# A fused two-layer kernel: the order of its instructions now comes from a list scheduler

## The chip, the cores and the metric

The kernel runs on one NeuronCore of a Trainium2 chip. The metric is the time of one execution on the device in microseconds (us); less is better. TensorE (PE) does the matrix products into PSUM banks, VectorE (DVE), ScalarE (ACT) and GpSimd (POOL) do elementwise work, and SyncE (SP) issues the DMA transfers. Each engine works through its own instructions in a fixed order; semaphores tie the engines together.

## The reference

Three steps on 16384 tokens (4 x 4096) of width 192:

```python
out = np.einsum('hk,bskhg->bshg', softmax(weight), x_unf)  # causal window of 7 taps, 8 heads of 24
h = x @ w_in                 # layer 1: 192 -> 2048
x = (h * np.cos(h)) @ w_out  # back to 192
h = np.maximum(x @ w_in2, 0) # layer 2, the same sizes
y = (h * h) @ w_out2
```

`x` is float32, the four weight matrices are float64.

## The kernel before, in words

Tokens are handled in `NB` = 32 blocks of `T` = 512 columns, the hidden width in `NC` = 16 chunks of 128. Every operand of a product is split into a high and a low part of the type float32r, and each product is done as high x high + high x low + low x high. The width 192 is cut into 128 + 64 rows (`P`, `R`).

One item is one chunk of one block in one layer. Its first products (IN) fill a PSUM bank `h`. In layer 1 ACT rounds it (`kf1`), DVE subtracts (`f1`), ACT takes the sine (`sin1`), DVE multiplies by `h` (`g1`), ACT casts the high part (`hi1`), and DVE or POOL subtracts the low part (`lo1`). In layer 2 ACT does relu, square and the cast (`relu2`, `sq2`, `hi2`) and DVE the low part (`lo2`). The second products (OUT) add the item into two banks `o`, which `evac` scales, splits and passes on (layer 1) or sends out (layer 2) once the block's 16 chunks are in.

The seven taps of a block (`conv_ops`) run on DVE; for block 0 they are shared with ACT and POOL. A chunk's weights are loaded and split in seven steps, `prep_m` to `prep_l`: bit masks and arithmetic on DVE (lines 181 to 183 and 194), the exponent on ACT, the product on POOL (200), the cast on ACT or DVE (206, 208, 209), the subtractions on POOL or DVE (219, 220, 226, 227).

Two kinds of TensorE instruction matter. An unpaired product (`mm_in`, `mm_out`, lines 293 to 303) uses all 128 rows of the array; an item costs 5 + 5 of them. A paired one (`MIX`, line 349) uses 64 rows, and two of them, for the lower and the upper half, run side by side; two items, one of each layer, cost 9 + 10 such pairs. The semaphore `turns` keeps the halves of one bank in order.

The order is written by hand: the string `START` up to the first product, then the lists of `PHASES`, one pass per step `s`. Steps 0 to 15 take block 0 through layer 1; from step 26 (`DEL`) layer 2 follows; from step 42 on `MIX` pairs one item of each layer, and after step 511 layer 2 goes on alone, unpaired, for its last 26 chunks. All weights are split before step 42.

Of the kernel before, what the change touches and what calls it, by code (L numbers as in the profile page):

```python
# [22 lines left out]
P = 128  # L23
# [4 lines left out]
DEL = 26  # L28
CUT = (320, 224)
SPLIT = ("A", "G")  # L30
BUFS = {"raw": 3, "s": 3, "m": 4, "k": 2, "g": 3, "r": 3, "g1": 3, "g2": 3, "o": 4, "h": 4}

START = (
    "X m@V:0 X Y X Y p:0 S X S Y s@V:0 S X Y S X S Y X w@V:0 m@V:1 Y S h@V:0 Y p:1 s@V:1 X S S Y "
    "d@V:0 l@V:0 m@V:2 S p:2 s:2 w@G:1 m@V:3 h:1 p:3 S S S d:1 l:1 w:2"
)

PHASES = (
    (
        0,  # L40
        "IN1:0 k1:0 s@V:-3 w@G:-3 f1:0 OUT1:2 h@A:-2 m:-4 hi1:1 F sin1:0 d:-2 p:-4 lo1@G:1 "
        "l:-2 g1:0",
    ),
    (
        16,
        "p:5 IN1:-2 s:-2 k1:-1 F d@G:-2 f1:-1 sin1:0 hi1:1 lo1@G:1 w@G:-1 OUT1:2 F l@G:-3 "
        "h@V:0 g1:0 m:3",
    ),
    (
        22,  # L50
        "w@G:-2 IN1:-1 k1:-1 f1:-1 F IN2:0 p:-3 relu2:0 hi1:1 h@V:-2 sq2:0 d@G:-2 sin1:-1 OUT1:2 m:-4 "
        "l@G:-2 s@V:-3 hi2:0 lo2@V:0 g1:0 lo1@G:1 OUT2:1",
    ),
    (
        42,
        "MIX k1:0 hi1:1 F Ea f1:0 relu2:-1 sin1:0 sq2:-1 hi2:0 lo2:0 lo1:1 hi2:-1 g1:0 F Es",
    ),
)


def f32(t):
    return t.bitcast(F32)


@with_exitstack
def tile_kernel(
# [22 lines left out]
    g_p = ctx.enter_context(tc.tile_pool(name="g", bufs=BUFS["g"]))
    r_p = ctx.enter_context(tc.tile_pool(name="r", bufs=BUFS["r"]))  # L90
    g1_p = ctx.enter_context(tc.tile_pool(name="g1", bufs=BUFS["g1"]))
    g2_p = ctx.enter_context(tc.tile_pool(name="g2", bufs=BUFS["g2"]))
    ps_h = ctx.enter_context(tc.tile_pool(name="ps_h", bufs=BUFS["h"], space=PSUM))
    ps_o = ctx.enter_context(tc.tile_pool(name="ps_o", bufs=BUFS["o"], space=PSUM))
# [60 lines left out]
    IH, OA, OX, IL, OL, IX = 0, P, 2 * P, 3 * P, 4 * P, 5 * P  # L155
    WC = 6 * P
    wts = [const.tile([P, NC, WC], F32R, name=f"wt{l}") for l in (1, 2)]
    srcs = (w1, w2)
    HALF = -1
    FULL = ((IH, "xh"), (IH, "xl"), (IL, "xh"), (IX, "yh"))  # L160
    U = 2 * D
    lower, upper = slice(0, R), slice(R, P)
    prep = {}

    def prep_load(u):

        l, c = divmod(u, NC)
        raw = raw_p.tile([P, U, 2], I32, tag="raw", name="raw")
        nc.sync.dma_start(raw[:, : P + D], srcs[l][c * P : (c + 1) * P, : P + D])
        for half, d in ((lower, c & ~1), (upper, c | 1)):  # L170
            row = d * P + c % 2 * R
            nc.sync.dma_start(raw[half, P + D :], srcs[l][row : row + R, P + D :])
        prep[u] = raw

    def prep_m(u, E=V):

        raw = prep[u]
        hi, lo = raw[:, :, 1], raw[:, :, 0]
# [12 lines left out]

    def prep_s(u, E=V):
        raw, s, m = prep[u]
        E.scalar_tensor_tensor(  # L194
            out=s, in0=raw[:, :, 1], scalar=-(2**31), in1=s, op0=ALU.bitwise_and, op1=ALU.bitwise_or
        )

    def prep_w(u, E=G):
        raw, s, m = prep[u]
        E.tensor_tensor(out=f32(m), in0=f32(m), in1=f32(s), op=ALU.mult)  # L200

    def prep_h(u, E=A):
        l, c = divmod(u, NC)
        w = f32(prep[u][2])
        t = wts[l][:, c, :]
        (E.copy if E is A else E.tensor_copy)(t[:, 0 : P + D], w[:, 0 : P + D])
        even, odd, x = rest(l, c)
        A.copy(even[lower, x], w[lower, P + D :])
        A.copy(odd[upper, x], w[upper, P + D :])

    def rest(l, c):
        x = IX + c % 2 * R
        return wts[l][:, c & ~1, :], wts[l][:, c | 1, :], slice(x, x + R)

    def prep_d(u, E=V):
        l, c = divmod(u, NC)
        w = f32(prep[u][2])
        even, odd, x = rest(l, c)
        E.tensor_tensor(out=even[upper, x], in0=w[lower, P + D :], in1=f32(even[lower, x]), op=ALU.subtract)
        E.tensor_tensor(out=odd[lower, x], in0=w[upper, P + D :], in1=f32(odd[upper, x]), op=ALU.subtract)  # L220

    def prep_l(u, E=G):
        l, c = divmod(u, NC)
        w = f32(prep.pop(u)[2])
        t = wts[l][:, c, :]
        E.tensor_tensor(out=t[:, IL:IX], in0=w[:, 0 : 2 * P], in1=f32(t[:, 0 : 2 * P]), op=ALU.subtract)
        E.tensor_tensor(
            out=t[:, OX + R : IL], in0=w[:, 2 * P : P + D], in1=f32(t[:, OX : OX + R]), op=ALU.subtract
        )


    xin = {}
    x1 = {}
    x2 = {}
    ready = [0, 0]

    def is_ready(l):
        ready[l] += 1

    def load_x(n):  # L240
        x = xin_p.tile([P, 2, T + PAD], F32, name="x")
        nc.sync.dma_start(x, xp[:, n])
        xin[n] = x[:, 0], x[:, 1]

    def conv_ops(n):

        src = xin.pop(n)
        parts = []
        ops = []
        for j in range(2):  # L250
            y = y_p.tile([P, T], F32, tag=f"y{j}", name=f"y{j}")
            h = x1_p.tile([P, T], F32R, tag=f"xh{j}", name=f"xh{j}")
            lo = x1_p.tile([P, T], F32R, tag=f"xl{j}", name=f"xl{j}")
            parts.append((h, lo))

            def tap(k, E=V, c=slice(0, T), y=y, j=j):
                xk = src[j][:, k + c.start : k + c.stop]
                wk = wtap[:, j, k : k + 1]
                if k == 0:
                    E.tensor_scalar(y[:, c], xk, wk, None, op0=ALU.mult)  # L260
                else:
                    E.scalar_tensor_tensor(out=y[:, c], in0=xk, scalar=wk, in1=y[:, c], op0=ALU.mult, op1=ALU.add)  # L262

            def both(k, tap=tap, cut=CUT[j], y=y, j=j):
                if cut < T:
                    xk = src[j][:, k + cut : k + T]
                    z = y[:, cut:] if k == 0 else r_p.tile([P, T], F32, tag="r", name="z")[:, cut:]
                    A.activation(z, xk, AF.Copy, scale=wtap[:, j, k : k + 1])
                    if k > 0:
                        G.tensor_tensor(out=y[:, cut:], in0=y[:, cut:], in1=z, op=ALU.add)  # L270
                if cut > 0:
                    tap(k, V, slice(0, cut))

            def last(y=y, h=h, lo=lo, c=SPLIT[0] if n == 0 else "V", d=SPLIT[1] if n == 0 else "V"):
                (A.copy if c == "A" else V.tensor_copy)(h, y)  # L275
                engines[d].tensor_tensor(out=lo, in0=y, in1=f32(h), op=ALU.subtract)  # L276

            f = both if n == 0 else tap
            ops += [lambda k=k, f=f: f(k) for k in range(K)] + [last]
        x1[n] = parts  # L280
        ops[-1] = lambda f=ops[-1]: (f(), is_ready(0))
        return ops


    def mm_in(h, l, c, parts, todo):
        w = wts[l][:, c, :]
        (xh, xl), (yh, yl) = parts
        for o, x, st, sp in todo:
            x = {"xh": xh, "xl": xl, "yh": yh, "yl": yl}[x]
            k = slice(0, P)  # L290
            if o == HALF:
# [381 lines left out]
```

## Time and profile before

| what | value |
|---|---|
| time, median of 3 runs | 2418.58 us (2416.64 to 2419.15) |
| the profiled execution: its time, its span | 2418.69 us, 2416.9 us |
| PE busy | 2318.7 us, 96% of the span |
| DVE busy, ACT busy, POOL busy | 1871.2, 1910.1, 158.3 us |
| chain that ended last | PE 90%, DVE 6%, ACT 2% of the span |

The span runs from the first instruction to the last. A share over the whole span mixes stages with different limits, so the rows below are read by stage: the opening up to about 261 us, the paired stretch, and the unpaired end from 2346 us.

### The profile page before, as it was taken

To read this page: it belongs to the slowest core of one execution; us is meant where nothing else is said; L and a number is where in the kernel's file an instruction comes from. 1 tells how busy PE (TensorE), PEld (TensorE's weight loads), DVE (VectorE), ACT (ScalarE), POOL (GpSimd) and SP (SyncE) were. 2 spreads that over 40 slices of the span, in tenths; PEclk is the share of its full clock that TensorE was granted. 3 is DMA by queue.
4 is the path that set the end of the run, shared out by engine and by line. 5 is a ranking of instruction groups with operands and counts; after the bars stand their busy time and mean duration, and the time that the engine had idled before them with its cause. 6 is when DMAs were issued, how large, how long until landed. Compare 5 with 4: busy or idle time off the path is not lost.

```text
span 2416.9 us, 45917 instructions
## 1 busy us (share of the span) xinstructions
PE 2318.7 (96%) x18682; PEld 1999.2 (83%) x18682; DVE 1871.2 (77%) x3036; ACT 1910.1 (79%) x3361; POOL 158.3 (7%) x186
## 2 busy tenths in 40 slices
PE   3578999999999999999999999999999999999999
PEld 2456788888888888888888888888888888888887
DVE  8988778777777887777888777788777778777653
ACT  4556788888888888888888888888888788888877
POOL 5557100000000000000000000000000000000000
PEclk8889999999999999999999999999999999999999
DMA  2211000000000000000000000000000000000000
GB/s 90 62 40 55 16 17 17 1 17 17 17 17 17 12 6 17 17 17 17 17 6 13 16 17 17 17 17 6 12 17 17 17 17 17 1 17 17 8 8 14
DMA packets 21859, 45.10 MB, mean 19 GB/s; under 512 B 3216, under 2 KB 7312, under 8 KB 21648
## 3 DMA queue, kind: packets, MB, share of 16 engines
q1 hardware_dynamic: 21648, 42.16, 5.7%
q8 instruction: 148, 2.42, 0.4%
q14 instruction: 63, 0.52, 0.1%
HBM read 29.56 MB, written 12.58 MB: 17 GB/s over the span
## 4 chain that ended last, share of the span: by engine, by line
PE 90%; DVE 6%; ACT 2%; issue 1%; POOL 0%; DMA 0%; ACTq 0%; DVEq 0%
PE o L349 45%; PE h L349 41%; PE h L293 2%; DVE y L262 1%; DVE g L466 1%; ACT k L452 1%; DVE raw_m L182 1%; DVE raw_s L194 1%; DVE gl L498 1%; DVE raw_s L181 1%; DVE k L458 0%; PE o L300 0%; PE o L302 0%; PE o L303 0%; PE o L301 0%
## 5 line engine op out<-in xcount | busy, mean ns | idle before, releaser
L349 PE MATMUL o<-gh,wt 64*128 64x512 f32 x5628 | 1008.7, 392 | 0.0
L349 PE MATMUL h<-xh,wt 64*128 64x512 f32 x2814 | 954.1, 392 | 3.0 <-DVE xh L275 1.8
L349 PE MATMUL h<-x2h,wt 64*128 64x512 f32 x1876 | 736.6, 393 | 0.7 <-ACT r L484 0.7
L349 PE MATMUL o<-gl,wt 64*128 64x512 f32 (+1 forms) x3752 | 700.9, 392 | 0.0
L452 ACT ACTIVATE k<-h,quarter 128x512 int32<-128x512 f32 x512 | 352.6, 689 | 427.4 <-PE h L349 342.3
L349 PEld LDWEIGHTS o<-gh,wt 64*128 64x128 f32 x5628 | 592.6, 184 | 94.4 <-issue 5.5
L458 DVE TENSOR_TENSOR k<-h,k 128x512 f32<-128x512 f32 x512 | 353.1, 690 | 352.7 <-ACT k L452 346.6
L349 PE MATMUL h<-xl,wt 64*128 64x512 f32 x1407 | 551.4, 392 | 0.2 <-DVE xl L276 0.2
L349 PEld LDWEIGHTS h<-xh,wt 64*128 64x128 f32 x2814 | 517.4, 184 | 36.9 <-DVE xh L275 2.2
L462 ACT ACTIVATE k<-k,right 128x512 f32<-128x512 f32 x512 | 369.2, 721 | 21.4 <-DVE k L458 21.3
L498 DVE TENSOR_TENSOR gl<-r,gh 128x512 fp32r<-128x512 f32 x512 | 353.3, 690 | 41.1 <-ACT gh L492 39.9
L349 PEld LDWEIGHTS h<-x2h,wt 64*128 64x128 f32 x1876 | 345.8, 184 | 45.9 <-ACT r L484 1.0
L349 PEld LDWEIGHTS o<-gl,wt 64*128 64x128 f32 (+1 forms) x3752 | 347.5, 158 | 42.8
L349 PE MATMUL h<-y2h,wt 64*128 64x512 f32 x938 | 368.5, 393 | 0.0
L349 PE MATMUL h<-x2l,wt 64*128 64x512 f32 x938 | 368.4, 393 | 0.0
L466 DVE TENSOR_TENSOR g<-k,h 128x512 f32<-128x512 f32 x512 | 348.7, 681 | 0.4
L492 ACT CAST gh<-r 128x512 fp32r<-128x512 f32 x512 | 317.8, 621 | 15.7
L477 DVE TENSOR_TENSOR gl<-g,gh 128x512 fp32r<-128x512 f32 x471 | 322.6, 685 | 0.0
L488 ACT ACTIVATE r<-r 128x512 f32<-128x512 f32 x512 | 320.4, 626 | 1.1
L471 ACT CAST gh<-g 128x512 fp32r<-128x512 f32 x512 | 312.7, 611 | 5.8 <-DVE g L466 5.6
L484 ACT ACTIVATE r<-h 128x512 f32<-128x512 f32 x512 | 308.0, 602 | 4.7 <-PE h L293 4.6
L262 DVE SCALAR_TENSOR_TENSOR y<-x,wtap,y 128x512 f32<-128x512 f32 (+1 forms) x384 | 295.1, 770 | 5.1
(90 smaller groups left out, 2100.4 us busy)
## 6 DMA issues: line engine op xcount, KB each, us to landing
x<-in_xp_dram SPq DMA_DIRECT2D x32, 518.0 KB, 3.7
raw<-in_w_dram SPq DMA_DIRECT2D x32, 320.0 KB, 2.9
out_dram<-ac SPq DMA_DIRECT2D x32, 256.0 KB, 2.0
out_dram<-bc SPq DMA_DIRECT2D x32, 128.0 KB, 2.3
raw<-in_w_dram SPq DMA_DIRECT2D x64, 32.0 KB, 2.6
w_sm<-in_wrep_dram SPq DMA_DIRECT2D x1, 7.0 KB, 1.7
```

Source lines behind the costliest of these rows:

```text
L262: E.scalar_tensor_tensor(out=y[:, c], in0=xk, scalar=wk, in1=y[:, c], op0=ALU.mult, op1=ALU.add)
L349: return nc.tensor.matmul(bank[0:m], w[k, o : o + m], x[k], start=st, stop=sp)
L452: A.activation(k, h_t[0, i], AF.Identity, bias=quarter)
L458: V.tensor_tensor(out=f, in0=h_t[0, i], in1=k, op=ALU.subtract)
L462: A.activation(tmp[i], tmp[i], AF.Sin, scale=2.0 * math.pi, bias=right)
L466: V.tensor_tensor(out=g, in0=tmp.pop(i), in1=h_t.pop((0, i)), op=ALU.mult)
L471: A.copy(h, tmp[i])
L477: E.tensor_tensor(out=lo, in0=tmp.pop(i), in1=f32(h), op=ALU.subtract)
L484: A.activation(r, h_t.pop((1, i)), AF.Relu)
L488: A.activation(tmp2[i], tmp2[i], AF.Square)
L492: A.copy(h, tmp2[i])
L498: E.tensor_tensor(out=lo, in0=tmp2.pop(i), in1=f32(h), op=ALU.subtract)
```

## The change: two blocks side by side, weights two chunks at a time, one scheduler

All work is now described as steps (`Step`) with a cost on each engine that may do it, the steps they follow, the buffers they take and free, and a due time. `Order.run` takes, over and over, the step that can start first on its engine by these costs, the earlier due one at a tie, and emits it. The costs are numbers in the code; the chip then works through what was emitted.

```diff
-DEL = 26
-CUT = (320, 224)
-START = (
...
-PHASES = (
...
+LEAD = 4
+EARLY = 3
+LAGS = (3, 2)
+BUFS = {"raw": 2, "s": 2, "m": 2, "x": 3, "t": 12, "g": 11, "h": 4, "o": 4, "xs": 4}
+PAIR, DRAIN, WAY = 233, 170, 90
...
+    def run(self):
...
+                    at = max(now, s.ready)
+                    for kind, n in s.takes:
...
+                        key = (at, s.due, s.seq)
+                        if pick is None or key < pick[0]:
+                            pick = key, s
```

A step of the weights now handles two chunks, 768 columns instead of 384, and all of its arithmetic is on DVE and ACT. A pair comes in by seven DMAs.

```diff
-    U = 2 * D
+    U = 2 * (P + D) + P
...
+        b = order.add(
+            "s" + name,
+            {"V": one(U)},
...
+            "p" + name,
+            {"A": act(U)},
...
+            "m" + name,
+            {"V": one(U)},
...
+            "f" + name,
+            {"V": two(U)},
...
+            "n" + name,
+            {"V": two(U)},
...
+            "w" + name,
+            {"V": two(U)},
...
+            "h" + name, {"A": act(U)}, lambda s, e: A.copy(w[:, HI : HI + U], f32(m())), (g2,), due=due - 2500
...
+        return order.add("l" + name, {"V": two(U) + 300}, low, (h,), frees=((d, "m"),), due=due - 1500)
```

The functions behind these names are those of before on wider tiles, and `low` makes three subtractions, of 640, 64 and 64 columns (lines 337, 340 and 341). Blocks 0 and 1 go through layer 1 together. A slot takes one item of the list `first` and one of `other`, pairs their first products (6 + 3 pairs) and the second products of two earlier items (5 + 5 pairs). Two items of one layer can now be a pair, since a pair needs an even and an odd chunk only.

```diff
+    first = [(0, 0)] + [(0, n) for n in range(2, NB)] + [(1, NB - 1)]
+    other = [(0, 1)] + [(1, n) for n in range(NB - 1)]
+    xs = [Item(l, n, c, i * NC + c) for i, (l, n) in enumerate(first) for c in range(NC)]
+    ys = [Item(l, n, c ^ 1, i * NC + c) for i, (l, n) in enumerate(other) for c in range(NC)]
...
+        if x < LEAD:
+            ins = (0, xs[x]), (0, xs[x + 1])
+            x += 2
+        elif x == late and y < late + LEAD:
+            ins = (1, ys[y]), (1, ys[y + 1])
+            y += 2
+        elif x == late and pend[0]:
+            pass
+        elif x < len(xs) and y < len(ys):
+            ins = (0, xs[x]), (1, ys[y])
+            x, y = x + 1, y + 1
...
+            {"V": 685, "G": pool(T)} if it.slot < 18 and it.n == 1 else {"V": 685},
...
+        p = product(f"IN{turn}", 6 if turn == 0 else 3, write, after, (("h", 2),) if turn == 0 else (), done)
...
+        p = product(f"OUT{turn}", 3 if x is y else 5, write, after, (("o", 2 * len(new)),) if new else (), frees)
```

On DVE, before, in the opening, one chunk's weights (`raw_s`, `raw_m`, `wt`) stand between the steps of one item at a time (`k` and `g`, with a tap `y`):

```order
L181 TENSOR_SCALAR raw_s<-raw 128x384
L182 TENSOR_SCALAR raw_m<-raw 128x384
L183 SCALAR_TENSOR_TENSOR raw_m<-raw,raw_m 128x384
L262 SCALAR_TENSOR_TENSOR y_266<-x,wtap,y_266 128x512
L219 TENSOR_TENSOR wt_108<-raw_m,wt_108 64x64
L220 TENSOR_TENSOR wt_108<-raw_m,wt_108 64x64
L466 TENSOR_TENSOR g<-k,h_473 128x512
L194 SCALAR_TENSOR_TENSOR raw_s<-raw,raw_s 128x384
L458 TENSOR_TENSOR k<-h_514,k 128x512
```

On DVE, now, at the fifth of the sixteen pairs of chunks (line 603 is the old `f1`, 617 the old `g1`, 648 the old `lo1` and `lo2`; `t` and `g` are shared buffers):

```order
L302 SCALAR_TENSOR_TENSOR m_72<-raw_68,m_72 128x768
L648 TENSOR_TENSOR g_90<-t_88,g_93 128x512
L311 SCALAR_TENSOR_TENSOR s_70<-raw_68,s_70 128x768
L603 TENSOR_TENSOR t_85<-h_100,t_85 128x512
L326 TENSOR_TENSOR m_72<-m_72,s_70 128x768
L603 TENSOR_TENSOR t_77<-h_101,t_77 128x512
L617 TENSOR_TENSOR t_86<-t_85,h_100 128x512
L648 TENSOR_TENSOR g_95<-t_81,g_94 128x512
L337 TENSOR_TENSOR wt_66<-m_72,wt_66 128x640
L340 TENSOR_TENSOR wt_66<-m_72,wt_66 128x64
L341 TENSOR_TENSOR wt_66<-m_72,wt_66 128x64
```

The product (326) and the large subtraction (337), which POOL did, now stand on DVE, twice as wide, and the steps of two items come between them.

On PE, before, in the opening, the second products of one chunk of block 0 follow the first products of another (`h`, `o` banks, `xh` and `xl` the parts of the block):

```order
L293 MATMUL h_555<-xh_140,wt_108 128x512
L293 MATMUL h_555<-xl_141,wt_108 128x512
L293 MATMUL h_555<-xh_140,wt_108 128x512
L293 MATMUL h_555<-xh_143,wt_108 128x512
L293 MATMUL h_555<-xl_144,wt_108 128x512
L299 MATMUL o_360<-gh_542,wt_108 128x512
L300 MATMUL o_360<-gl_549,wt_108 128x512
```

On PE, now, in an early slot, the halves of two items alternate, here in the second turn of the first products and the start of the second products (`xs` 108 to 111 are the parts of block 0, 112 to 115 those of block 1):

```order
L411 MATMUL h_101<-xs_112,wt_66 128x512
L411 MATMUL h_100<-xs_108,wt_66 128x512
L411 MATMUL h_101<-xs_113,wt_66 128x512
L411 MATMUL h_100<-xs_109,wt_66 128x512
L411 MATMUL h_101<-xs_112,wt_66 128x512
L411 MATMUL h_100<-xs_108,wt_66 128x512
L411 MATMUL o_106<-g_96,wt_66 128x512
L411 MATMUL o_104<-g_90,wt_66 128x512
```

Each product of before is now half of a pair with a product of another block, on the same pair of weight chunks.

## Rows read from the trace of the kernel before

**Rows 1.** Busy time by stage: stretch, its length, each engine, PEclk, DMA.

```profile
0.00:30.00 30.00, 2.83 (x4) 1.34 (x5) 26.65 (x59) 11.78 (x26) 16.32 (x24) 1.00 0.36 115
30.00:140.00 110.00, 70.41 (x224) 49.94 (x224) 100.75 (x155) 63.17 (x128) 61.24 (x63) 0.84 0.17 52
140.00:261.00 121.00, 97.15 (x355) 71.04 (x353) 94.56 (x158) 76.40 (x159) 80.74 (x100) 0.92 0.16 47
261.00:294.00 33.00, 30.62 (x245) 25.76 (x247) 25.33 (x42) 24.28 (x43) 0.00 (x0) 0.95 0.10 29
294.00:2346.00 2052.00, 2052.00 (x17580) 1798.52 (x17576) 1597.14 (x2585) 1682.14 (x2920) 0.00 (x0) 1.00 0.05 14
2346.00:2417.00 71.00, 65.69 (x282) 52.56 (x280) 26.77 (x41) 52.35 (x88) 0.00 (x0) 1.00 0.04 12
```

**Rows 2.** The chain that ended last: start, length, engine, tile, line, count.

```profile
2344.99 1.17 PE o L349 x10
...
2411.45 0.25 PE o L303
...
2412.99 0.68 DVE bc L426
```

**Rows 3.** Groups of instructions, mostly of the weights: count, busy, mean ns, idle.

```profile
L200 POOL TENSOR_TENSOR raw_m<-raw_m,raw_s 128x384 f32<-128x384 f32 x31 | 32.3, 1043 | 28.8 <-DVE raw_s L194 28.8
...
L226 POOL TENSOR_TENSOR wt<-raw_m,wt 128x256 fp32r<-128x256 f32 x31 | 27.3, 882 | 3.1 <-ACT wt L206 1.8
L194 DVE SCALAR_TENSOR_TENSOR raw_s<-raw,raw_s 128x384 int32<-128x384 int32 x32 | 24.7, 771 | 0.0
L183 DVE SCALAR_TENSOR_TENSOR raw_m<-raw,raw_m 128x384 f32<-128x384 uint32 x32 | 22.3, 696 | 1.1
...
L182 DVE TENSOR_SCALAR raw_m<-raw 128x384 int32<-128x384 int32 x32 | 20.4, 639 | 0.0
L419 ACT COPY sw<-bc 64x512 f32<-64x512 f32 x32 | 19.8, 620 | 0.4
...
L181 DVE TENSOR_SCALAR raw_s<-raw 128x384 int32<-128x384 int32 x32 | 16.4, 513 | 0.0
```

**Rows 4.** DVE in order of time in the opening: start, length, instruction.

```profile
86.86 1.42 DVE L182 TENSOR_SCALAR raw_m<-raw 128x384 int32<-128x384 int32 x1
...
92.96 0.35 DVE L181 TENSOR_SCALAR raw_s<-raw 128x384 int32<-128x384 int32 x1
93.23 0.36 DVE L182 TENSOR_SCALAR raw_m<-raw 128x384 int32<-128x384 int32 x1
93.62 0.56 DVE L183 SCALAR_TENSOR_TENSOR raw_m<-raw,raw_m 128x384 f32<-128x384 uint32 x1
94.09 1.77 DVE L262 SCALAR_TENSOR_TENSOR y<-x,wtap,y 128x512 f32<-128x512 f32 x1
```

**Rows 5.** POOL in order of time, the same stretch.

```profile
86.68 1.38 POOL L477 TENSOR_TENSOR gl<-g,gh 128x512 fp32r<-128x512 f32 x1
```

**Rows 6.** DVE in order of time in the paired stretch.

```profile
1002.24 0.68 DVE L498 TENSOR_TENSOR gl<-r,gh 128x512 fp32r<-128x512 f32 x1
...
1003.44 0.68 DVE L466 TENSOR_TENSOR g<-k,h 128x512 f32<-128x512 f32 x1
1004.04 1.53 DVE L262 SCALAR_TENSOR_TENSOR y<-x,wtap,y 128x512 f32<-128x512 f32 x2
```

**Rows 7.** PE alone in short stretches: length, busy (count), PEclk, DMA.

```profile
78.00:82.00 4.00, 3.82 (x9) 0.50 0.31 88
285.00:287.00 2.00, 0.50 (x2) 0.95 0.00 0
287.00:289.00 2.00, 1.88 (x10) 0.50 0.00 0
289.00:291.00 2.00, 2.00 (x16) 0.70 0.00 0
```

**Rows 8.** DMA issues on the page: KB each, us to landing.

```profile
x<-in_xp_dram SPq DMA_DIRECT2D x32, 518.0 KB, 3.7
```

More of the change, by code (lines that the diff above doesn't have):

```diff
@@ L1 @@
+import heapq
 import math
-from collections import deque
 from contextlib import ExitStack
@@ new lines, with __init__, add, open @@
+class Order:
+    def __init__(self):
+        self.steps = []
+        self.free = {}
+        self.hold = {}
+    def add(self, *a, **k):
+        s = Step(*a, **k)
+        s.seq = len(self.steps)
+        self.steps.append(s)
+        return s
+    def run(self):
+        for s in self.steps:
+            s.left = len(s.after)
+            for a in s.after:
+                a.next.append(s)
+        ready = {}
+        for s in self.steps:
+            if not s.left:
+                self.open(ready, s)
+        clock = {}
+        done = 0
+        while done < len(self.steps):
+            best = None
+            for e, todo in ready.items():
+                now = clock.get(e, 0.0)
+                pick = None
+                for s in todo:
+                    if s.end is not None:
+                        continue
+                    at = max(now, s.ready)
+                    for kind, n in s.takes:
+                        have = self.free[kind]
+                        if len(have) < n:
+                            break
+                        at = max(at, have[n - 1][0] + WAY)
+                    else:
+                        key = (at, s.due, s.seq)
+                        if pick is None or key < pick[0]:
+                            pick = key, s
+                if pick and (best is None or pick[0] < best[0]):
+                    best = pick[0], pick[1], e
+            assert best, [s.name for todo in ready.values() for s in todo if s.end is None][:40]
+            (at, _, _), s, e = best
+            cost = s.costs[e]
+            s.end = at + cost
+            clock[e] = s.end - {"P": DRAIN, "N": s.end}.get(e, 60)
+            for kind, n in s.takes:
+                have = self.free[kind]
+                s.got[kind] = [t for _, _, t in have[:n]]
+                del have[:n]
+            s.emit(s, e)
+            for what, kind in s.frees:
+                for t in what.got[kind]:
+                    self.count += 1
+                    self.free[kind].append((s.end, self.count, t))
+                self.free[kind].sort()
+            for x in s.costs:
+                ready[x].remove(s)
+            done += 1
+            for n in s.next:
+                n.left -= 1
+                n.ready = max(n.ready, s.end + s.way)
+                if not n.left:
+                    self.open(ready, n)
+        return max(s.end for s in self.steps)
+    count = 0
+    def open(self, ready, s):
+        for e in s.costs:
+            ready.setdefault(e, []).append(s)
@@ L211, in rest @@
[L211 to L228, printed above, removed]
-        )
@@ L232, in tile_kernel @@
[L232 to L282, printed above, removed]
@@ new lines, in tile_kernel, with ordered @@
+    fence = [None]
+    def ordered():
+        last = {}
+        for g in groups:
+            for owner, rows in g.uses:
+                before = last.get(owner)
+                if before is not None and before[1] is not rows:
+                    b = before[0]
+                    assert b < g.at
+                    if b + 1 < g.at:
+                        want = b + 1, 0
+                    else:
+                        groups[b].ends = True
+                        want = b, 1
+                    g.wait = max(g.wait or want, want)
+            for owner, rows in g.uses:
+                last[owner] = g.at, rows
@@ new lines, in small @@
+    def small():
+        for _ in softmax():
+            yield
+    steps = small()
+    taps = None
+    next(steps)
+    for i in range(21):
+        taps = order.add(
+            f"softmax{i}", {"V": 260 if i else 2600}, lambda s, e: next(steps, None), (taps,), due=-50000, way=0
+        )
+    first = [(0, 0)] + [(0, n) for n in range(2, NB)] + [(1, NB - 1)]
+    other = [(0, 1)] + [(1, n) for n in range(NB - 1)]
+    xs = [Item(l, n, c, i * NC + c) for i, (l, n) in enumerate(first) for c in range(NC)]
@@ new lines, in tile_kernel, with start_of @@
+    SLOT = 19 * PAIR
+    def start_of(s):
+        return 24000.0 + s * SLOT + min(s, 18) * 1800 + max(0, min(s, 34) - 18) * 1000
+    preps = {}
+    blocks = {}
+    for s, (ins, _, _) in enumerate(slots):
+        for it in ins:
+            preps.setdefault((it.l, it.c // 2), s)
+            blocks.setdefault((it.l, it.n), s)
+    weights = {}
+    for (l, u), s in preps.items():
+        weights[l, u] = prep(l, u, start_of(s))
+    for (l, n), s in blocks.items():
+        if l == 0:
+            conv(n, start_of(s))
@@ L635, in _twice @@
+    with tc.manual_schedule():
+        order.run()
 def _twice(a):
```

846 lines of the change are left out of this document (480 added, 366 removed).

## The prediction

> **What bounds the kernel now.** I read the busy time by stage first. The reader is to see one long stretch, 294 to 2346 us, in which PE is busy for 2052.00 of 2052 us at full clock, with DVE at 78% and ACT at 82%; and two ends that look otherwise [rows 1]. Up to 261 us DVE is the busiest engine (92% between 30 and 140 us) while PE has long gaps and its granted clock means 0.84 and 0.92; the last 71 us are PE again. Second comes the chain of waits: in the long stretch ten halves, five pairs, take 1.17 us, so a pair costs 0.2333 us [rows 2]. The unpaired products at the end cost the same each: 282 in 65.69 us [rows 1]. So the unit of PE's work is 0.2333 us, and one unpaired product or one pair is one unit.
>
> The kernel before needs 860 unpaired products and 469 steps of 19 pairs: 860 + 8911 = 9771 units, 2280 us. The span is 2416.9, so 137 us are lost. The opening holds 583 units (4 + 224 + 355 records [rows 1]), 136 us of work in 261: 125 us lost. In the 33 us from 261 on PE does 245 halves, 28.6 us of work, and loses 4.4, around 286 [rows 1, 7], and 5.2 us lie behind the last product at 2411.70 [rows 2]. Only the opening has much to give.
>
> **The change part by part.** *Fewer units.* 1024 items of 9.5 pairs are 9728; twelve items whose second products go out alone (slots 3, 5, 498 to 500, 513 to 515) take 6 units, not 5: 9740 in all. That is 31 units less, 7 us.
>
> *The weights.* One operation now does two chunks. Free of POOL, a DVE operation with one tensor of 384 columns lets the next start after 0.27 us, and one with two tensors after 0.47 [rows 4]; with 512 columns it is 0.60 (two operations in 1.20) [rows 6], so about 1.0 ns per column. For 768 columns I take 0.50 and 0.86, for the subtraction of 640 columns 0.73, and for each of 64 at most 0.27. A pair of chunks costs DVE 2 x 0.50 + 3 x 0.86 + 0.73 + 2 x 0.27 = 4.85 us, sixteen pairs 78. Before, the four DVE operations alone cost 2 x (0.513 + 0.639 + 0.696 + 0.771) = 5.24 us per pair, and POOL's product and large subtraction 2 x (1.043 + 0.882) = 3.85 more [rows 3]. The four take 2.72 now: the rows of before are lengthened by POOL. While POOL works at 86.68 [rows 5], a mask on DVE takes 1.42 us, and 0.36 at 93.23 [rows 4].
>
> That is a place to weigh a rule. The Trainium skill (GPSIMD Engine Reference, section Engine selection) calls GpSimd about twice as slow as VectorE for elementwise work with two inputs; by that alone POOL's 3.85 us would come to DVE as 1.9 and the opening would be about 31 us of DVE work longer. The same page's Specifications say that the two engines share SBUF interfaces. The trace agrees with the second: by its rows DVE's work per pair falls, POOL's share included, from 5.24 to 4.85.
>
> *The opening.* DVE sets it, so I count DVE's instructions in the new order up to the last subtraction of the sixteenth pair. They are the 78 us of weights; 49 `f`, 48 `g` and 43 low parts, 140 x 0.60 = 84; 48 taps at 0.68 (between 0.60 and 0.77, two in 1.53 [rows 6]) and 8 first taps at 0.4 (between 0.27 and 0.60), 36; 8 low parts of blocks and 7 steps of `evac` and casts, 9; 23 small softmax operations under 0.27 each, 5. Together 212 us. POOL still makes 16 low parts. Each may lengthen DVE by nothing up to 1.07 us (1.42 - 0.35), 0 to 17 in all; DVE operations that read PSUM and one SBUF tensor stand among them, so I take 0.4 each, 6. DVE's waits are the open size. The nearest row is 30 to 140 us with 100.75 busy of 110, 8% idle [rows 1], with one item in flight; two items at once give DVE other work while ACT has one of them, so I take 5%, between nothing and 8%. With 2.5 us before the first operation (DVE is idle for 3.35 of the first 30 us [rows 1]): 218 / 0.95 + 2.5 = 232 us. At that point 49 layer-1 items have their first products, so PE stands in slot 30 and has done 556 units, 130 us. The opening loses 102 us, not 125.
>
> First products: PE can start behind the first weights and the taps of block 0, about 24 us. The first transfer of weights is now 524 KB; one of 518 KB lands in 3.7 us [rows 8], and DVE has the softmax for so long. Later ones have a second buffer and some 12 us per pair; without that cover each would cost up to 4 us.
>
> *The rest.* 9740 - 556 = 9184 units at 0.2333 are 2142.9 us. In slot 498 block 31 enters layer 2 right behind its own last second product: a copy, two swaps of 0.62 [rows 3], an addition, a cast and a subtraction of up to 0.6 to 0.7 each [rows 6] with the handing over, 4.2 us, less the four products that need no low part; 3.5 us stay. PE then restarts slower: behind such a gap 26 halves ran in 4 us [rows 7] where 34 fit, so 1 us more, 4.5 in all (the like of the 4.4 us of before, around 286). When a block ends, two banks must be emptied in the six pairs before the next second products, 1.4 us; two operations of 0.6 to 0.7, one of them perhaps in progress, just about fit. I take 0.05 us for 62 of them, 3 us (between 0 and 0.4 each). Behind the last product 5.2 us as before, and 0.5 for the single products ahead of it.
>
> Sum: 232 + 2142.9 + 4.5 + 3 + 5.7 = 2388 us of span. The profiled execution took 1.8 us more than its span (2418.69 against 2416.9) and is within 0.1 us of the median: **2390 us**, 1.2% faster.
>
> **The rivals.** *DVE hardly waits (2369).* The scheduler fills every hole and POOL costs nothing: 212 + 2.5 = 214, and no wait at the banks: 2142.9 + 214 + 10.2 + 1.8 = 2369. For it: two items and a pair of chunks are nearly always at hand. Against it: costs in the code can differ from the chip's, and an engine's order is fixed.
>
> *PE's clock bounds the opening (2428, slower).* PE has gaps in the opening, and after a gap its granted clock is 0.50, the lower level of 1.2 GHz: 9 products in 3.82 us, 0.42 each [rows 7]. If the 538 units after block 1's parts are ready (DVE row 77, about 44 us by the same durations) run like that, slot 30 is reached at 44 + 538 x 0.42 = 270 instead of 232: 2142.9 + 270 + 13.2 + 1.8 = 2428. It decides from 0.35 us a unit on, and makes the kernel slower than before from 0.40 on (slot 30 at 261). Against it: the mean unit in the opening of before was 170.4 us / 583 = 0.29, and with PE busy for 3.88 of the 4 us from 287 to 291 the clock shows 0.50, then 0.70, and full further on [rows 1, 7]; a PE that is the bound has no gaps. The Trainium skill (TensorE: Matmul & The Clock Gate, section HAM oscillation) has this as its rule: bursts between waits each start at half clock, so the price is paid every time. The trace agrees that it is paid, not that it lasts.
>
> *The long stretch gets waits (2438, slower).* The order there is now the scheduler's. If in each of the 478 slots from 34 on one operand comes 0.1 us late, that is 48 us. From 0.06 us on it eats the whole gain. For it: conv taps and `evac` now stand anywhere between the steps of the items. Against it: DVE and ACT have 18 to 22% to spare [rows 1] while PE shows no gap there, with the same four banks for first products and the same lags of three and two steps between first and second products.
>
> **How the numbers follow.** Chances: forecast 0.64, DVE hardly waits 0.20, clock 0.08, long stretch 0.08. Runs of this kernel tell about 0.2%, 5 us, from no change. The forecast's own spread is 2376 (no waits on DVE with POOL's 6) to 2408 (8% waits, POOL's 17); 0.95 of it is faster, the first rival wholly, the other two hardly: faster 0.81, same 0.05, slower 0.14. The range for 8 in 10 takes in the first rival and the forecast, and reaches to no change: 2368 to 2416.
>
> **What would show it.** Right: PE starts near 24 us, DVE is over 90% busy up to about 230 us with almost no POOL, mask operations of 768 columns last 0.5 to 0.6 us, and slot 30 comes at 220 to 245. From there PE is busy without a break except once, near 2330 us, for about 4 us. Wrong: PE clock near 0.5 over most of the opening with PE busy; DVE waiting over a tenth of it for ACT; PE idle in the long stretch at every slot or every block end.

## The result and the profile after

The kernel after takes 2387.07 us (median of 4 runs, 2385.93 to 2388.41), the kernel before beside it 2417.61 us: a ratio of 0.9873, 95% interval 0.9856 to 0.9891. The forecast was 2390. The profiled execution of after has a span of 2385.6 us, 31.3 less than before.

Busy time by stage of the kernel after, with the columns of [rows 1]:

```profile
30.00:140.00 110.00, 81.28 (x536) 61.68 (x536) 107.94 (x162) 69.70 (x111) 18.73 (x12) 0.92 0.18 52
140.00:261.00 121.00, 110.20 (x860) 99.43 (x858) 116.29 (x194) 98.37 (x168) 10.91 (x4) 0.93 0.19 56
261.00:294.00 33.00, 33.00 (x286) 32.78 (x284) 24.60 (x40) 26.92 (x47) 0.00 (x0) 1.00 0.00 1
```

DVE is busy for 107.94 of 110 us between 30 and 140, where it was for 100.75. The gap of before around 286 is gone (286 halves in 33 us, was 245). All products are halves of pairs now, so two records are one unit of 0.2333 us. The same view for PE alone gives the loss, which is the time less 0.2333 us for each unit done in it:

```profile
0.00:261.00 261.00, 196.29 (x1408) 0.93 0.21 63
...
261.00:2296.00 2035.00, 2035.00 (x17446) 1.00 0.05 13
2296.00:2320.00 24.00, 20.93 (x129) 0.86 0.06 17
2320.00:2366.00 46.00, 46.00 (x398) 1.00 0.01 1
2366.00:2381.00 15.00, 13.83 (x88) 1.00 0.09 27
...
2304.00:2308.00 4.00, 3.91 (x20) 0.50 0.02 4
```

1408 halves are 704 units, 164.3 us: the opening loses 96.7 us, before 125.4. (Before did 581 units up to 261 us; the prediction's 583 is the sum of three rows, in which the two records that cross an edge count twice.) From 261 to 2296 nothing is lost (17446 halves are 2035.4 us). From 2296 to 2320 only 64.5 units are done, so 9.0 us go there; from 2366 to the last product, at 2380.46, 4.2 more. The whole difference is then 28.7 us of opening, and 10.0 us of units (9771 before, 9728 now), less 7.5 us that after loses more behind 261 (13.9, before 6.4): 31.2 of the 31.3.

The stop, on PE in order of time (start, length, instruction, count, and in brackets the idle time ahead with what ended it):

```profile
2296.37 1.46 PE L411 MATMUL o<-g,wt 64*128 64x512 f32 x10
2299.54 0.50 PE L411 MATMUL h<-xs,wt 64*128 64x512 f32 x2 [1.72 <-DVE xs L710]
2300.27 0.73 PE L411 MATMUL h<-xs,wt 64*128 64x512 f32 x4 [0.22 <-DVE xs L715]
2301.33 0.79 PE L411 MATMUL h<-xs,wt 64*128 64x512 f32 x2 [0.33 <-DVE xs L729]
2302.53 1.22 PE L411 MATMUL h<-xs,wt 64*128 64x512 f32 x4 [0.41 <-DVE xs L734]
```

Four parts of block 31 arrive one after the other, and PE does a few halves with each. Then PE runs slower: in 2304 to 2308 it is busy for 3.91 us at a granted clock of 0.50, with 20 records, and at 0.98 in the next 4 us. The end, on the chain that ended last:

```profile
2372.33 0.98 PE o L411 x4
2373.30 0.04 issue
2373.34 0.98 PE o L411 x4
...
2379.49 0.98 PE o L411 x4
```

A second product that goes out alone (here the last four) has two turns, each of about 1.02 us for what would be 2.5 units, 0.58 us. [Rows 2] showed no such pieces: before, the end was unpaired.

### The profile page after: what moved, and what is told of

Read it like the earlier page. It is cut to its first block, busy times and chain, and to the rows that moved or that the text cites. A ratio compares the mean times of both kernels' runs of the same rounds, so it can differ in the third digit from the quotient of the medians.

```text
span 2385.6 us, 46741 instructions
## 1 busy us (share of the span) xinstructions
PE 2312.1 (97%) x19456; PEld 2253.4 (94%) x19456; DVE 1843.3 (77%) x3001; ACT 1911.7 (80%) x3278; POOL 30.0 (1%) x22
## 4 chain that ended last, share of the span: by engine, by line
PE 93%; DVE 5%; SPq 1%; ACT 0%; issue 0%; DMA 0%; POOL 0%; DVEq 0%; ACTq 0%; POOLq 0%
PE o L411 49%; PE h L411 44%; DVE t L378 1%; DVE t L603 1%; DVE t L617 1%; DVE g L648 0%; DVE m L302 0%; DMA raw<-in_w_dram 0%; DVE s L311 0%; SPq L259 0%; DVE wt L337 0%; DVE m L326 0%; DVE s L270 0%; ACT t L591 0%; DVE m L288 0%
## 5 line engine op out<-in xcount | busy, mean ns | idle before, releaser
L411 PE MATMUL o<-g,wt 64*128 64x512 f32 x10240 | 1514.6, 394 | 5.5 <-DVE g L648 2.5
L411 PE MATMUL h<-xs,wt 64*128 64x512 f32 x9216 | 1400.1, 396 | 62.9 <-ACT xs L393 27.5
L411 PEld LDWEIGHTS o<-g,wt 64*128 64x128 f32 x10240 | 1224.5, 185 | 38.4 <-PE o L411 9.3
L411 PEld LDWEIGHTS h<-xs,wt 64*128 64x128 f32 x9216 | 1161.7, 186 | 88.2 <-ACT xs L393 28.0
L648 DVE TENSOR_TENSOR g<-t,g 128x512 fp32r<-128x512 f32 x1008 | 689.0, 684 | 57.1 <-PE o L411 28.2
L643 ACT CAST g<-t 128x512 fp32r<-128x512 f32 x1024 | 625.7, 614 | 116.7 <-DVE t L617 115.5
L603 DVE TENSOR_TENSOR t<-h,t 128x512 f32<-128x512 f32 x512 | 351.3, 687 | 340.8 <-ACT t L591 340.6
L591 ACT ACTIVATE t<-h,quarter 128x512 int32<-128x512 f32 x512 | 350.6, 688 | 238.0 <-PE h L411 237.8
L617 DVE TENSOR_TENSOR t<-t,h 128x512 f32<-128x512 f32 x512 | 348.9, 683 | 116.4 <-ACT t L610 112.8
L610 ACT ACTIVATE t<-t,right 128x512 f32<-128x512 f32 x512 | 364.5, 714 | 27.3 <-DVE t L603 26.4
L636 ACT ACTIVATE t<-t 128x512 f32<-128x512 f32 x512 | 323.3, 635 | 10.3
L648 POOL TENSOR_TENSOR g<-t,g 128x512 fp32r<-128x512 f32 x16 | 29.6, 1853 | 133.6 <-ACT g L643 127.9
L278 ACT ACTIVATE s<-s 128x768 int32<-128x768 int32 x16 | 13.5, 842 | 12.9 <-DVE s L270 12.8
```

The source lines that it names most:

```text
L411: return nc.tensor.matmul(bank, w[k, o : o + P], x[k], start=st, stop=sp)
L591: lambda s, e: A.activation(s.got["t"][0].bitcast(I32), h(), AF.Identity, bias=quarter),
L603: lambda s, e: V.tensor_tensor(out=t(), in0=h(), in1=t().bitcast(I32), op=ALU.subtract),
L610: lambda s, e: A.activation(t(), t(), AF.Sin, scale=2.0 * math.pi, bias=right),
L617: lambda s, e: V.tensor_tensor(out=s.got["t"][0], in0=t(), in1=h(), op=ALU.mult),
L636: lambda s, e: A.activation(a.got["t"][0], a.got["t"][0], AF.Square),
```

## The experiments

All in one table. The two columns of losses are us in the profiled execution, up to 261 us and from there to the last product. The kernel before was 2416.4 to 2417.0 us beside these runs, 0.6 to 1.2 below the 2417.61 beside after, so a difference of 1 us from after says nothing.

| kernel | time, us | ratio to before, 95% | lost to 261 | lost behind |
|---|---|---|---|---|
| before | 2417.61 | | 125.4 | 6.4 |
| after | 2387.07 | 0.9873 (0.9856-0.9891) | 96.7 | 13.9 |
| 1 no GpSimd | 2380.27 | 0.9849 (0.9834-0.9863) | 91.5 | 13.3 |
| 2 product on GpSimd | 2379.68 | 0.9847 (0.9832-0.9861) | 89.3 | 14.1 |
| 3 first mask twice | 2391.84 | 0.9898 (0.9881-0.9914) | 99.7 | 13.5 |
| 4 one block after the other | 2376.07 | 0.9832 (0.9817-0.9847) | 85.0 | 14.4 |
| 5 half-width steps | 2388.84 | 0.9881 (0.9867-0.9894) | 99.6 | 13.5 |
| 6 cast twice | 2389.98 | 0.9887 (0.9874-0.9901) | 99.2 | 14.1 |
| 7 as 4, lone products merged | **2359.96** | 0.9764 (0.9750-0.9777) | 80.1 | 4.1 |
| 8 as 7, product on GpSimd | 2365.71 | 0.9786 (0.9773-0.9800) | 85.3 | 4.1 |
| 9 as 1, lone products merged | 2376.93 | 0.9836 (0.9823-0.9849) | 90.6 | 9.3 |
| 10 before, no GpSimd | 2409.46 | 0.9969 (0.9958-0.9981) | 115.6 (to 250) | 6.8 |

**1. No work on GpSimd.** The sixteen low parts of block 1 go to DVE.

```diff
-            {"V": 685, "G": pool(T)} if it.slot < 18 and it.n == 1 else {"V": 685},
+            {"V": 685},
```

> The 16 low parts that POOL makes in the opening go to DVE (0.60 us each there, 9.6 in all); nothing else is changed by hand. By the prediction's price each of them lengthens DVE by 0.4 us through POOL, so the exchange costs 16 x 0.2 = 3 us: about 2390. By the changed kernel's own rows (the groups of the weights and the taps on DVE are together 13 us longer in the opening than free of POOL, 0.8 us per POOL operation) it gives 16 x 0.2 = 3 us back: about 2384. If DVE doesn't bound the opening: 2387, within 1 us.

Measured: 6.8 us faster than after (some 6 by the ratios to before), so DVE with sixteen more operations reaches the end of the opening sooner: the sixteenth pair's last subtraction ends at 226.0 us, in after at 230.5. Groups of DVE instructions up to 235 us (count, busy us, mean ns, idle ahead), first of after:

```profile
L378 DVE SCALAR_TENSOR_TENSOR t<-x,wtap,t 128x512 f32<-128x512 f32 x48 | 37.8, 806 | 0.0
L603 DVE TENSOR_TENSOR t<-h,t 128x512 f32<-128x512 f32 x50 | 33.5, 682 | 2.0 <-ACT t L591 1.7
...
L648 DVE TENSOR_TENSOR g<-t,g 128x512 fp32r<-128x512 f32 x46 | 32.5, 709 | 1.1 <-ACT g L643 1.0
L302 DVE SCALAR_TENSOR_TENSOR m<-raw,m 128x768 f32<-128x768 uint32 x16 | 18.5, 1157 | 0.0
L311 DVE SCALAR_TENSOR_TENSOR s<-raw,s 128x768 int32<-128x768 int32 x16 | 16.3, 1017 | 0.0
...
L270 DVE TENSOR_SCALAR s<-raw 128x768 int32<-128x768 int32 x16 | 12.7, 795 | 3.8 <-DMA raw<-in_w_dram 3.8
L288 DVE TENSOR_SCALAR m<-raw 128x768 int32<-128x768 int32 x16 | 9.9, 621 | 0.0
...
L340 DVE TENSOR_TENSOR wt<-m,wt 128x64 fp32r<-128x64 f32 x16 | 4.6, 286 | 0.0
```

and of this experiment:

```profile
L648 DVE TENSOR_TENSOR g<-t,g 128x512 fp32r<-128x512 f32 x65 | 44.0, 685 | 0.2 <-ACT g L643 0.2
L378 DVE SCALAR_TENSOR_TENSOR t<-x,wtap,t 128x512 f32<-128x512 f32 x48 | 34.8, 741 | 0.0
L603 DVE TENSOR_TENSOR t<-h,t 128x512 f32<-128x512 f32 x51 | 34.1, 683 | 0.8 <-ACT t L591 0.7
...
L311 DVE SCALAR_TENSOR_TENSOR s<-raw,s 128x768 int32<-128x768 int32 x16 | 15.2, 949 | 0.0
L302 DVE SCALAR_TENSOR_TENSOR m<-raw,m 128x768 f32<-128x768 uint32 x16 | 15.2, 949 | 0.0
...
L288 DVE TENSOR_SCALAR m<-raw 128x768 int32<-128x768 int32 x16 | 8.8, 552 | 0.0
L270 DVE TENSOR_SCALAR s<-raw 128x768 int32<-128x768 int32 x16 | 8.8, 552 | 4.1 <-DMA raw<-in_w_dram 4.1
...
L340 DVE TENSOR_TENSOR wt<-m,wt 128x64 fp32r<-128x64 f32 x16 | 3.5, 218 | 0.0
```

The same instructions are longer in after: 16 x (0.208 + 0.068 + 0.243 + 0.069 + 0.068) + 48 x 0.065 + 46 x 0.024 = 14.7 us, 0.92 for each of the sixteen on GpSimd. They spare DVE 16 x 0.60 = 9.6. DVE's busy time up to that last subtraction says the same: 219.0 us in after, 214.3 here. Line 603, which reads one operand from PSUM, is not longer (682 ns, here 683).

**2. The weights' product on GpSimd as well.** Sixteen operations of 768 columns leave DVE.

```diff
-            {"V": two(U)},
-            lambda s, e: V.tensor_tensor(out=f32(m()), in0=f32(m()), in1=f32(b.got["s"][0]), op=ALU.mult),
+            {"G": pool(U)},
+            lambda s, e: G.tensor_tensor(out=f32(m()), in0=f32(m()), in1=f32(b.got["s"][0]), op=ALU.mult),
```

> The product of the weights (16 of 768 columns) goes back to POOL, as in the kernel before. DVE loses 16 x 0.87 = 14 us. By the prediction's price (0.4 us per 1.47 us of POOL, 0.27) POOL's 16 x 2.1 = 33 us lengthen DVE by 9: about 2382. By the changed kernel's rows (0.8 per 1.85 us, 0.43) by 14: about 2387. If the chain of a pair's steps bounds the opening (POOL's product is 1.2 us longer than DVE's, sixteen times), up to 2405.

Measured: 2379.68, the same as 1 and 7.4 us faster than after. GpSimd makes 16 products (2.24 us each) and 15 low parts. The groups of DVE, as above, up to 235 us:

```profile
L378 DVE SCALAR_TENSOR_TENSOR t<-x,wtap,t 128x512 f32<-128x512 f32 x48 | 41.1, 875 | 0.0
L648 DVE TENSOR_TENSOR g<-t,g 128x512 fp32r<-128x512 f32 x51 | 39.6, 783 | 0.0
...
L302 DVE SCALAR_TENSOR_TENSOR m<-raw,m 128x768 f32<-128x768 uint32 x16 | 16.9, 1053 | 0.0
...
L270 DVE TENSOR_SCALAR s<-raw 128x768 int32<-128x768 int32 x16 | 11.4, 712 | 4.9 <-DMA raw<-in_w_dram 4.9
L288 DVE TENSOR_SCALAR m<-raw 128x768 int32<-128x768 int32 x16 | 10.2, 640 | 0.0
L340 DVE TENSOR_TENSOR wt<-m,wt 128x64 fp32r<-128x64 f32 x16 | 9.4, 585 | 0.0
```

Against 1 they are longer by 48 x 0.134 + 51 x 0.098 + 16 x (0.104 + 0.160 + 0.088 + 0.367) = 22.9 us, and GpSimd spares DVE 15 x 0.60 + 16 x 0.87 = 22.9. So the same time as without it is what these rows give, and beside the low parts the wide product pays for itself where they don't: it adds 8 us of lengthening to the 14.7 of after, and spares 13.9. By itself, in experiment 8, it doesn't.

**3. One operation more per pair of chunks.** The first mask of the weights is written twice.

```diff
-            lambda s, e: V.tensor_scalar(s.got["s"][0], raw(1), 0x7FF00000, None, op0=ALU.bitwise_and),
+            lambda s, e: [
+                V.tensor_scalar(s.got["s"][0], raw(1), 0x7FF00000, None, op0=ALU.bitwise_and) for _ in (0, 1)
+            ],
```

> The first mask of every pair of chunks is written twice on DVE (16 more operations of 768 columns, 0.47 us each from start to start; same result, same order otherwise). If DVE bounds the opening the kernel is 7 to 8 us longer: 2394 to 2395. If PE at its lower clock or the chains between ACT and DVE bound it, DVE's 5% of waits take it up: 2387 to 2390.

Measured: 4.8 us slower than after. Sixteen such operations at 0.47 us from one start to the next are 7.5 us, so about two thirds are paid, fewer than the 7 to 8 expected. In the profiled execution, 2 us faster than the median, the last subtraction ends 3.6 us later (234.1); DVE is busy for 8.3 us more and idle for 4.8 less. So DVE is the bound of the opening in the main, and part of an addition goes into its waits.

**4. One block after the other.** Layer 1 of block 0, then of block 1, and layer 2 from item 26 on, as before; the scheduler and the steps of two chunks stay, GpSimd is left out as in 1.

```diff
-LEAD = 4
+LEAD = 26
...
-    first = [(0, 0)] + [(0, n) for n in range(2, NB)] + [(1, NB - 1)]
-    other = [(0, 1)] + [(1, n) for n in range(NB - 1)]
+    first = [(0, n) for n in range(NB)]
+    other = [(1, n) for n in range(NB)]
...
-    late = len(xs) - NC
+    late = None
...
+        elif y < len(ys):
+            ins = (1, ys[y]), (1, ys[y + 1])
+            y += 2
```

> Blocks 0 and 1 go through layer 1 one after the other, layer 2 follows 26 items behind, as in the kernel before; scheduler, weights two chunks at a time and pairs stay, and POOL makes no low parts. The end has 36 single second products more (36 units, 8 us, and their waits). Opening: DVE's work up to the sixteenth pair of chunks is 193 us for 520 units done. If DVE is kept as busy as in the changed kernel (95%), the pair comes at 206 us and the opening loses 85 us, 11 less than in the changed kernel: one block at a time is no worse, and the kernel takes some 2395 to 2402 for its end alone. If the second block is what keeps DVE busy, DVE falls to 88%, the pair comes at 222 and the opening loses 101 or more: 2410 to 2420.

Measured: 4.2 us faster than 1, and the opening alone loses 6.5 us less. Up to 261 us 1509 halves are done, in 1 1453 and in after 1408. That two blocks go side by side isn't where the gain is from.

**5. Half-width steps.** Each wide step of the weights as two of half the columns, here the first; the others likewise.

```diff
-            lambda s, e: V.tensor_scalar(s.got["s"][0], raw(1), 0x7FF00000, None, op0=ALU.bitwise_and),
+            lambda s, e: [
+                V.tensor_scalar(s.got["s"][0][:, c], raw(1)[:, c], 0x7FF00000, None, op0=ALU.bitwise_and) for c in cols
+            ],
```

> The changed kernel, with each DVE step of the weights written as two operations of half the columns (96 more operations in 16 pairs; order otherwise the same). One mask of 768 columns lets the next start after 0.47 us in the changed kernel, two of 384 after 2 x 0.27 in the kernel before; with two tensors 0.87 against 2 x 0.47: 0.07 more per step. If DVE bounds the opening and width is worth only that: 96 x 0.07 = 7 us more, about 2394. If doing two chunks at a time were most of the 29 us that the opening gained: 2400 or more. If width is worth nothing: 2387.

Measured: 1.8 us slower than after, not clear of the scatter (2386.5 to 2389.8 in four runs, after 2385.9 to 2388.4); in the profiled execution 2.9 more are lost up to 261. The 96 more operations keep DVE busy for 6.1 us more up to the last subtraction (225.1 us), of which its idle time takes up 2.8. It splits only the wide steps: the subtractions of 64 columns, 96 before and 32 now, stay as they are.

**6. The cast on ACT twice.**

```diff
-            "h" + name, {"A": act(U)}, lambda s, e: A.copy(w[:, HI : HI + U], f32(m())), (g2,), due=due - 2500
+            "h" + name, {"A": act(U)}, lambda s, e: [A.copy(w[:, HI : HI + U], f32(m())) for _ in (0, 1)], (g2,), due=due - 2500
```

> The changed kernel, with ACT's cast of the weights' high part written twice (16 more operations of 0.83 us on ACT, same result). ACT is busy for 70 of the 110 us from 30 on, so if DVE alone bounds the opening it is hidden: 2387 to 2389. If the chains that go back and forth between DVE and ACT bound it, each cast delays the subtraction behind it: 16 x 0.75 = 12 us, up to 2399.

Measured: 2.9 us slower than after. Of ACT's 13 us more about 3 reach the end: up to the last subtraction DVE is as busy as in after (218.8 us) and idles 3.2 us longer, and its waits for this cast grow from 0.9 to 6.3 us. ACT isn't the bound, but not wholly hidden.

**7. Lone second products merged.** Experiment 4, and two second products of one block that would each go out alone share one group.

```diff
+        if len(outs) == 1:
+            for k in (0, 1):
+                if pend[k] and pend[k][0].slot + LAGS[k] < s + (not ins):
+                    outs.append(pend[k].pop(0))
+                    break
...
-        if x is y:
+        same = x.key is y.key
+        if same:
...
-                a, b = x.second(turn), x.second(1 - turn)
+                a = [m for it in outs for m in it.second(turn)]
+                b = [m for it in outs for m in it.second(1 - turn)]
...
-        p = product(f"OUT{turn}", 3 if x is y else 5, write, after, (("o", 2 * len(new)),) if new else (), frees)
+        p = product(f"OUT{turn}", 3 * len(outs) if same else 5, write, after, (("o", 2 * len(new)),) if new else (), frees)
```

> The blocks one after the other as in e4, and two single second products of one block are written as one group, so that a bank's halves change over half as often. In e4's end the slots take 5.40 us for 21 units (4.90) nine times, and the last three lose 3.9 us: 8 us of waits at the change-over. Half of them go: 2372, and 2368 if the wait is paid only once per slot. If the loss in e4's end is not these waits: 2376. The opening is the same.

Measured: 16.1 us faster than 4, twice what was expected at most. The chain that ended last, in a late stretch of 4:

```profile
2313.70 1.40 PE h L411 x8
...
2317.07 0.04 issue
2317.11 0.98 PE o L411 x5
2318.09 0.04 issue
...
2319.10 1.17 PE h L411 x10
```

and of this experiment:

```profile
2324.56 1.06 PE o L411 x9
2325.62 0.10 PE h L411
2325.73 0.13 PE o L411
...
2328.99 1.06 PE o L411 x9
```

With lone products a round of two items takes 5.40 us (2313.70 to 2319.10), with merged ones 4.43 (2324.56 to 2328.99), which is 19 units. Each "issue" of 0.04 us stands at a change of halves in the lone groups, where the turn is 0.98 us and not 0.58. So a lone second product costs no sixth unit but a wait at each of its turns. By the table 10.3 us of the gain are behind 261 and 4.9 in the opening, which has lone products at its start too; that these are the cause there is argued, not tried.

**8. Merged, with the product on GpSimd.** The edit of 2 on top of 7.

> e7 with the product of the weights on POOL (16 operations of 768 columns). e1 and e2 together price a low part on POOL at +0.4 us net and so the sixteen products on POOL at -5 us: e7 less 5, about 2366. With one block at a time DVE has less other work while POOL's product is under way (2.1 us instead of 0.9): if that wait is not covered, 16 x 1.2 = 19 us at most against it, up to 2385.

Measured: 5.7 us slower than 7, 5.2 of it up to 261 us. A product takes 2.14 us on GpSimd where DVE needs 0.96, and DVE's waits for ACT ahead of line 603 (611 in these two) are 3.1 us up to 225 us, not 0.4. And DVE is not less busy without the sixteen products: 187.0 us up to the last subtraction, 185.5 in 7, with 11.6 us idle and not 7.9. So the product's time on DVE comes back as lengthening of its other instructions, and the waits come on top. That the later product is what makes them wait wasn't tried by itself.

**9. Side by side, merged.** The merging that is shown for 7, on top of 1.

> The kernel after with all weight and activation steps on VectorE (as in the run without GpSimd work, 2380.3 us) and with the two lone second products of one block merged into one group of products. Theory (the end of the kernel loses about 0.3 to 0.44 us at each change between the halves of TensorE, and the opening side by side loses more than one block after the other): the merge saves 3 to 5 us of the twelve lone turns, so 2375 to 2377 us, 15 us above the version with one block after the other and the same merge (2360.0). Rival (the merge alone carried that version, and side by side costs nothing): 2360 to 2364 us.

Measured: 2376.93, 3.3 us less than 1 and 17.0 more than 7. By the table 10.5 of these are lost up to 261 and 5.2 behind it, where block 31 still stops PE; in 7 layer 2 runs 26 items behind and PE does 17446 halves between 261 and 2296 and 208 in the next 24 us, without a stop. So theory and number agree: what two blocks side by side change is a loss. The stretch around block 31's stop loses 6.0 us here, 8.8 in 1 and 9.3 in after (all records counted by their starts, 30 us from 2290 on); so some 3 us of it were lone products.

**10. The kernel before without GpSimd.** Its hand-written order stays; each step that GpSimd did stands on DVE at the same place. The taps of block 0, in which ACT and GpSimd had a share, are wholly on DVE (`CUT`).

```diff
-CUT = (320, 224)
-SPLIT = ("A", "G")
+CUT = (512, 512)
+SPLIT = ("A", "V")
...
-    def prep_w(u, E=G):
+    def prep_w(u, E=V):
...
-    def prep_l(u, E=G):
+    def prep_l(u, E=V):
```

The `@G` in the lists of the order are `@V` likewise.

> The kernel before with its hand-written order kept, and every step that GpSimd did (weights' products, some low parts) put on VectorE at the same place of the order. Theory (what the kernel before lost in the opening is VectorE's waiting in the hand-written order, 39 us idle of 261, and not the sharing with GpSimd): VectorE's work becomes about 249 us (some 70 us added, some 43 us of lengthening by GpSimd gone), so the sixteenth pair comes at 262 us if it then waits 5% and the time is the same, 2418 us; if the waits of the order stay at 15% it is up to 2448 us. Rival (GpSimd's share is the main thing that the kernel before lost): faster, 2400 us or less.

Measured: 6.9 us faster than the before beside it (2416.37); neither the theory's "the same or slower" nor the rival's 2400. DVE's waits up to 262 us (what was waited for, us in total, times, longest), of before:

```profile
DVE k L458 <- ACT k L452: 23.4, 31, 1.6
DVE gl L498 <- ACT gh L492: 9.4, 9, 1.6
```

and of this experiment:

```profile
DVE gl L498 <- ACT gh L492: 5.8, 6, 1.9
DVE k L458 <- ACT k L452: 3.3, 10, 0.8
```

Of 33 us of waiting 9 are left, and 2.5 new ones at line 477; the work from GpSimd now stands where DVE waited, and DVE's own instructions get their short times back (the masks 356 and 355 ns, 513 and 639 in [rows 3]). DVE is busy for 232.5 of 250 us when 576 units are done, before for 222.0 of 261 at 581. So of the 29 us that the opening gained, 10 (7 by the medians) are to be had in the old order by leaving GpSimd out.

## Why the prediction was right, point by point

**The bound.** "DVE sets it": shown in the main. DVE is busy for 95% of the time up to the sixteenth pair in after, an operation more costs 4.8 of 7.5 us (3), and leaving DVE alone brings 6.8 (1). Thirteen us more on ACT cost 2.9 (6), so a part of DVE's waits is ACT's.

**DVE's work.** 218 us were forecast up to the sixteenth pair and some 219 measured (220.5 busy up to 232 us), but by two errors against each other. DVE's own work was some 204 us, not 212, and GpSimd's sixteen operations lengthened DVE by 0.92 us each, not the 0.4 that was taken from between 0 and 1.07. Both ends of that bound came from rows. The argument for the value in between was right in itself, for the readers of PSUM kept their times (line 603 in 1); others, as the first mask and line 302, paid more than was thought (0.243 and 0.208 us in the mean of sixteen). The rule of the Trainium skill that spoke for GpSimd (GPSIMD Engine Reference, section Engine selection: about twice as slow as VectorE in elementwise work with two inputs) is not what decides here: 1853 ns stand against 685 for the same 512 columns, 2.7 times, and what GpSimd takes from DVE at the same time weighs more.

**The waits and the end of the opening.** 5% waits were taken, with 2.5 us ahead of DVE's first operation apart from them. Up to 230.5 us DVE idles 11.5 us, of which 2.5 are those: 9.0 of 228, 4%. DVE in order of time in after, the first masks of two pairs and the sixteenth pair's last subtraction among it:

```profile
7.21 0.56 DVE L270 TENSOR_SCALAR s<-raw 128x768 int32<-128x768 int32 x1 [2.00 <-DMA raw<-in_w_dram]
...
13.15 0.56 DVE L270 TENSOR_SCALAR s<-raw 128x768 int32<-128x768 int32 x1 [1.83 <-DMA raw<-in_w_dram]
...
230.26 0.24 DVE L341 TENSOR_TENSOR wt<-m,wt 128x64 fp32r<-128x64 f32 x1
```

The last one ends at 230.5, forecast 232. A mask of 768 columns lasts 0.56 us and lets the next start after 0.47 (0.5 to 0.6 and 0.50 forecast). PE starts at 24.9 (24 forecast) and is 24 units further at 232 us than was counted: 1161 records, 580 units, not 556. So the opening loses 96.7 us, forecast 102. DVE waits for the first two transfers of weights, 2.00 and 1.83 us; the softmax covers them in part only.

**The units.** "Twelve items take 6 units, not 5" failed. They take 5 and a wait of about 0.44 us at each turn (7). The 0.5 us forecast ahead of the last product was 4.2.

**The bank hand-over.** 3 us were taken (between 0 and 24); it is 0: 17446 halves in 2035.00 us of PE at full clock.

**Block 31.** The mechanism was right, four parts one after the other behind its own last product and then the lower clock; the size was 4.5 and the stretch loses 9.0, with the six lone products of these slots in it. With these merged it still loses 6.0 (9), so the stop itself was taken too small as well. It stands at 2298, not "near 2330": that place was guessed, and the sum doesn't rest on it.

**The sum.** Against the forecast of 2388 us of span: opening 5.5 us less, units 2.8 less, hand-over 3 less, block 31 4.5 more, lone products at the end 3.7 more: 2385, measured 2385.6. The terms are off by 19.5 us in all and cancel to 3, so that the number lies within 3 us is in part luck.

**The rivals.** *DVE hardly waits* (2369) asked for GpSimd at no cost, and that failed: 0.92 us each. Without GpSimd the kernel is at 2380, with the waits as they are. *PE's clock bounds the opening* (2428): the clock means 0.92 and 0.93 over the stages in which it was to be 0.50. The rule of the Trainium skill (TensorE: Matmul & The Clock Gate, section HAM oscillation) that each burst behind a wait starts at half clock is seen behind block 31's stop, 0.50 in 2304 to 2308, and it is paid once there. *The long stretch gets waits* (2438): PE has none from 261 to 2296.

**What carried the gain.** From before to after the opening gains DVE's idle time: 39.0 of 261 us at 581 units in before, 11.5 of 232 at 580 in after. DVE's busy time stays (222.0 and 220.5 us), though most of GpSimd's work is on it now. Without GpSimd on both sides, experiments 10 and 4 show the two parts apart:

| kernel | units done | time, us | DVE busy | DVE idle |
|---|---|---|---|---|
| before | 581 | 261 | 222.0 | 39.0 |
| 10 before, no GpSimd | 576 | 250 | 232.5 | 17.5 |
| 4 one block after the other | 578 | 220 | 208.1 | 11.9 |

So in the old order the waits fall by 21.5 us once GpSimd's work is DVE's own, and from 10 to 4 there are 24.4 us less work on DVE and only 5.6 less waiting. The groups of the weights' instructions add up to 116.1 us on DVE in 10 and 83.2 in 4. Of the 33, 14 are the 64-column subtractions in a third of the number (21.0 and 6.9 us), 5.5 are casts that ACT does now, and some 13 the wide steps; instructions overlap, so the time spared is less. Only the wide steps were tried by themselves (5, 2 to 3 us); the rest stands on these rows alone, and no run has the scheduler's order with the old steps, so what the order brings by itself stays open. Two blocks side by side and GpSimd's share, the visible parts of the change, cost 17 us (9 against 7; 4 while lone products stay, 1 against 4) and 7 us (1). The best version, 7, has neither, shares groups between lone products besides, and is 27.1 us faster than after.

## What to carry to other kernels

Where VectorE binds and GpSimd shares its work, compare the same instructions' durations with and without GpSimd before giving it any: here it took 14.7 us to spare 9.6, and 22.9 to spare 22.9. A scheduler's gain is found by following the binding engine, its busy and its idle time at equal work done, and not the features that came with it; turn each off alone. Groups of products that are ordered by semaphores among themselves want a partner of the same length, even one of their own block.

## What the runs showed of the hardware that was not expected

A GpSimd subtraction of 128 x 512 lasts 1.85 us beside DVE (0.685 there). With sixteen of them in the opening the first mask of 768 columns on DVE takes 0.795 us and not 0.552, the second 0.621 (means of sixteen, whether GpSimd ran beside them or not). DVE operations with one operand in PSUM (lines 603 and 617) keep theirs: 0.682 and 0.678, without GpSimd 0.683 and 0.680. Half products of one group and of the next run side by side, so a single half need not cost a unit. In 7, on PE in order of time at a change of halves:

```profile
2337.61 1.33 PE L411 MATMUL o<-g,wt 64*128 64x512 f32 x9
2338.63 0.39 PE L411 MATMUL h<-xs,wt 64*128 64x512 f32 x1
2338.78 0.39 PE L411 MATMUL o<-g,wt 64*128 64x512 f32 x1
2338.86 1.47 PE L411 MATMUL h<-xs,wt 64*128 64x512 f32 x10
```

The last half of `o` starts 0.15 us behind the first of `h`, beside it. A turn of a lone second product takes 0.98 to 1.02 us for 0.58 us of work.
